# Three y writes on ScalarE's queue, one product placed behind a table, and other counts of dummy matmuls, in a three-layer token-mixing kernel

## The chip, the cores and the metric

One NeuronCore of a Trainium2 chip runs the whole program. Its engines are TensorE (PE), VectorE (DVE), ScalarE (ACT), GpSimd (POOL) and SyncE (SP, which here only issues DMAs). The metric is the device time of one execution in microseconds. A profiled execution also has a span, from its first to its last instruction.

## What is computed

Three layers follow each other, for batch 4, sequence 768, model width 384 (8 heads of 48):

```
# 1. linear attention with a decaying state, per batch and head
for t in range(S):
    y[t] = r[t] @ (state + outer(u * k[t], v[t]))
    state = w[:, None] * state + outer(k[t], v[t])
# 2. gated MLP that mixes over the sequence
h = gelu(x @ w_in);  u, v = halves of h;  v_n = layernorm(v) * g_ln
x = x + (u * (w_sg @ v_n + b_sg)) @ w_out
# 3. gated causal convolution
gate = sigmoid(sum of 5 shifted x * conv_w);  out = (gate * (x @ w_val)) @ w_out2
```

## The kernel before

The attention is done in 24 chunks of 128 tokens (6 per batch, `NCH`). Within a chunk the sum over earlier tokens is a masked score matrix; between chunks a state T is carried. Powers of the decay w stand in two tables: `tabR` weighs r and `tabK` weighs k. `tables()` builds them at the start: DVE scans powers of w and of 1/w, 64 columns long; POOL multiplies the first half of a table by its last column to get the second half (line 352 for `tabK`). From the transposed `tabK` comes `tabS`, which weighs the k that go into the state.

Of one chunk, r and k are loaded (`ld`, lines 524 to 530), v too (`lv`). POOL forms k times `tabS` (`kS`), and r times k (`dv`), then times u; DVE sums that over the head's width (`dd`), POOL multiplies v by the sum (`D`): this is the token's own term. PE transposes r and k into PSUM, DVE and ACT evacuate them (`rT`, `kT`), PE makes the scores (`S_products`, line 669) and the state's update (`KV`), and DVE masks the scores and adds to T, which ACT decays (line 720). At last PE adds three products into y (`att_Y`). For chunk 0, r times k is not in the planner's hands: `dv0` (line 587) is called in `tables()`.

y stands with channels in partitions, 112 rows with a gap. `x_rows` (line 887) brings it into the order that the MLP wants: ACT copies it from PSUM (line 900), two DMAs write its two halves to DRAM (`write`, lines 904 and 905, 48 rows of four runs of 512 bytes each), and one DMA reads it back (`read`, line 910). For batch 0 the MLP starts on each chunk when it is read back: ACT rounds it to a high part and DVE subtracts for a low part (lines 984 and 988, `X`), and the V product of that chunk can run.

The MLP's products are each three matmuls of high and low parts (`three`, lines 1091 to 1093). Its weights come as 64-bit words that ACT, DVE and POOL turn into those parts (`prepare`, lines 379 to 405, the "words" and "win" rows of the trace). `w_sg` goes through sums of squares, a scale and transposing DMAs (line 497) before the mixing product over the sequence (`mlp_SG`) can start.

The order of every engine's instructions is written out when the program is built. A planner keeps a time for each engine and for the DMA engines; each step of a chain has engines it may go to and a planned cost, and the step that can start first goes next (`next_step`), with priorities for ties. "Q" is the DMA queue: its steps all go to `nc.sync`, in the order of the planned times; for Q steps of low priority the planner keeps no more than `AHEAD` of transfer time in front. `small` is the load of `g_ln` and `b_sg` (lines 316 and 318); it may go once the r and k of chunk `AFTER_SM` are in.

Where the planner foresees that PE waits in the first 30 us, `go` puts in dummy matmuls of ones (line 222), as many as fit into the planned wait; `FILLS` can replace the count of the n-th such place. More dummies follow the first scores and the first y, and `LAST_FILL` of them follow the last product of the program. Dummies write a PSUM tile that nobody reads.

Of the kernel before, what the change touches and what calls it, by code (L numbers as in the profile page):

```python
# [24 lines left out]
Q = P // 2  # L25
# [7 lines left out]
class Kern:  # L33
# [145 lines left out]
    def go(self, streams, choose):  # L179
# [3 lines left out]
        while True:  # L183
# [9 lines left out]
            if n is None:  # L193
# [7 lines left out]
                if n:  # L201
                    self.fill(FILLS.get(self.n_fill, n))
                    self.n_fill += 1
# [116 lines left out]
    def tables(self):  # L320

        nc = self.nc
        M = Q
        self.tabR = self.const([HR, NP, P], F32, "tabR")
        self.tabK = self.const([HR, NP, P], F32, "tabK")
        self.W = self.const([HR, NP], F32, "W")
        q = self.Rst(F32)[:HR, 0:NP * (Q + 1)].rearrange("d (p n) -> d p n", p=NP)
        wq, rw = (self.const([HR, NP], F32, n) for n in ("wq", "rw"))
        t = self.Rst(F32)[:HR]
        z, y, e = (t[:, n * NP * M:(n + 1) * NP * M].rearrange("d (p n) -> d p n", n=M) for n in range(3))  # L330
        nc.gpsimd.memset(z, 0.0)
        nc.gpsimd.memset(q[:, :, 0:1], 1.0)


        nc.vector.tensor_scalar(wq, self.wP, W_LEAST, W_MOST, ALU.max, ALU.min)

        def scan(src, dst):
            for p in range(NP):
                nc.vector.tensor_tensor_scan(dst[:, p], src[:, p:p + 1].to_broadcast([HR, M]), z[:, p], 1.0, ALU.mult, ALU.add)

        scan(wq, q[:, :, 1:])
        nc.scalar.copy(self.tabR[:, :, 0:M], q[:, :, 0:M])
        nc.gpsimd.tensor_mul(self.tabR[:, :, M:], q[:, :, 0:M], q[:, :, M:].to_broadcast([HR, NP, M]))
        nc.vector.reciprocal(rw, wq)
        scan(rw, y)


        nc.vector.scalar_tensor_tensor(e, q[:, :, 1:], -1.0, y, ALU.mult, ALU.mult)
        nc.vector.scalar_tensor_tensor(self.tabK[:, :, 0:M], e, 2.0, y, ALU.add, ALU.mult)

        def second(e):
            e.tensor_mul(self.tabK[:, :, M:], self.tabK[:, :, 0:M], self.tabK[:, :, M - 1:M].to_broadcast([HR, NP, M]))
            e.tensor_mul(self.W, q[:, :, M:].rearrange("d p o -> d (p o)"), q[:, :, M:].rearrange("d p o -> d (p o)"))

        self.dv0(nc.gpsimd)
        second(nc.gpsimd)
        self.mark("tabS0", T_S)

# [313 lines left out]
    def S_products(self, i):  # L672
        nc = self.nc
        rT, kT = self.kr[i]
        pA, pB = self.ps_a(), self.ps_a()
        for p in range(NP):
            for ps, r0 in ((pA, 0), (pB, 64)):
                nc.tensor.matmul(ps[:, p * P:(p + 1) * P], kT[r0:r0 + D, p, :], rT[r0:r0 + D, p, :], start=True, stop=True)
        self.mark(("S", i))
        if not i:  # L680
            self.fill(12)
        mb = self.mask.unsqueeze(1).to_broadcast([P, NP, P])
        parts = self.scores[i] = []
        for n, ps in enumerate((pA, pB)):

            def masked(e, ps=ps):
                t = self.wp.tile([P, NP, P], F32, tag="sc", name=self.nm("sc"), bufs=2)
                e.tensor_mul(t, ps.rearrange("s (p t) -> s p t", t=P), mb)
                parts.append(t)

            self.chain(("sc", i, n), ("V", 602.0, masked, ["sc"], ["pa"]), after=[("Y", i - 1)] if i else [], prio=pr(i))
# [199 lines left out]
    def x_rows(self, i, py):  # L891

        b, c = divmod(i, NCH)
        scr = self.xd[i]
        half, q = divmod(c, 3)
        x = {}

        def evac(e):
            x["y"] = self.wp.tile([HR, NP, P], F32, tag="yT", name=self.nm("yT"), bufs=NY)
            e.copy(x["y"], py.rearrange("d (p t) -> d p t", t=P))  # L900

        def write(e):
            dst = scr.rearrange("(p j e) t -> j e p t", p=NP, j=2)
            e.dma_start(dst[0], x["y"][0:D])
            e.dma_start(dst[1], x["y"][64:HR])

        def read(e):
            if q == 0:
                self.new_xf(b, half)
            e.dma_start(self.xf[b, half][:, :, KC - 1 + q * P:KC - 1 + (q + 1) * P], scr.rearrange("(m c) t -> c m t", c=P))  # L910

        self.chain(
            ("y", b, c),
            ("A", 500.0, evac, ["yT"], ["pa"]), ("Q", (2, 600), write, [], ["yT"]), ("Q", (1, 600), read, [] if q else ["xf"]),
            after=[("y", b, c - 1)] if q else [], prio=0,
        )
        if q == 0:
            self.x_parts(b, half)
# [333 lines left out]
    def mlp_O2(self, b, half, q, dst=None):  # L1252
# [13 lines left out]
        if b == B - 1 and half:  # L1266
            if q == 2:
                pz = self.ps_m()
                for _ in range(LAST_FILL):
                    nc.tensor.matmul(pz[:, 0:P], self.onesb, self.onesb, start=True, stop=True)  # L1270
# [182 lines left out]
def pr(i):  # L1453

    return 0 if i < NCH else PR_A if i >= 2 * NCH or i < FROM_B else PR_B
# [6 lines left out]
FROM_B, PR_B = 9, 2.5  # L1462
RAW, PR_RAW = 13, 2.5
QUAD, PAST_NS = 6, 520
AFTER_SG, AFTER_SM, AFTER_CW = 6, 6, 9
WA, WM = 4, 4
NW = 3
NR, NS, NA, NX, NY, NL, NV, NPA = 12, 10, 3, 3, 2, 3, 2, 4
# [16 lines left out]
BODY = "U10 S00 U11 S01 U12 S02 U13 S03 O00 O01 O02 S10 S11 A00 A01 A02 S12 S13 P00 O10 P01 O11 P02 O12 v0 A10 u00 A11 v1 A12 v2 u01 u02 v3 u03 P10 v4 P11 P12 v5"  # L1485
END = "U10 S00 U11 S01 U12 S02 U13 S03 O00 O01 S10 S11 O02 S12 S13 A00 A01 A02 O10 O11 O12 P00 P01 A10 A11 A12 P02 P10 P11 P12"
LATER = ['a', 'a', 'a', 'a', 'a', 'a']
FILLS = {}
LAST_FILL = 5
W_LEAST, W_MOST = 0.75, 1.0  # L1490
N_OK = HR * NP

# [41 lines left out]
```

## Time and profile before

| | before |
|---|---|
| median of 3 runs | 434.7 us (433.62 to 434.74) |
| profiled execution, its time | 432.49 us |
| profiled execution, its span | 430.7 us |
| PE busy, share of the span | 411.3 us, 96% |
| DVE busy | 346.6 us, 80% |
| ACT busy | 207.1 us, 48% |
| POOL busy | 208.9 us, 49% |
| mean granted TensorE clock | 0.996 of full speed |
| packets of SP's DMA queue, share of 16 DMA engines | 46.5% |

Times of day within the span are in microseconds from its first instruction. A busy time is the union of an engine's instructions; dummies count as busy PE. Idle time before an instruction is put down to what released it last. Issuing a DMA occupies the engine whose queue issues it (SPq, ACTq), and is not counted as busy; its landing is counted from the start of the issue.

### The profile page before, as it was taken

To read this page: it belongs to the slowest core of one execution; us is meant where nothing else is said; L and a number is where in the kernel's file an instruction comes from. 1 tells how busy PE (TensorE), PEld (TensorE's weight loads), DVE (VectorE), ACT (ScalarE), POOL (GpSimd) and SP (SyncE) were. 2 spreads that over 40 slices of the span, in tenths; PEclk is the share of its full clock that TensorE was granted. 3 is DMA by queue.
4 is the path that set the end of the run, shared out by engine and by line. 5 is a ranking of instruction groups with operands and counts; after the bars stand their busy time and mean duration, and the time that the engine had idled before them with its cause. 6 is when DMAs were issued, how large, how long until landed. Compare 5 with 4: busy or idle time off the path is not lost. (4 is left out here: it accounts for less than half of the span.)

```text
span 430.7 us, 11575 instructions
## 1 busy us (share of the span) xinstructions
PE 411.3 (96%) x4616; PEld 346.9 (81%) x4616; DVE 346.6 (80%) x740; ACT 207.1 (48%) x439; POOL 208.9 (49%) x243
## 2 busy tenths in 40 slices
PE   7988998889999999999999999899999999999996
PEld 7776787857787999877887999777878989776896
DVE  6887899987899788788989799777786696649992
ACT  2546667754464486534253486532132763104152
POOL 6776976466267657673597757652110322100000
PEclk9999999989999999999999999999999999999999
DMA  6998997699646716764558541632002001000012
GB/s 164 204 237 190 256 274 188 129 198 204 171 87 133 195 47 152 175 163 107 126 124 211 148 113 37 176 84 55 20 2 91 18 2 55 2 0 2 0 38 79
DMA packets 128955, 50.15 MB, mean 116 GB/s; under 512 B 90752, under 2 KB 126720, under 8 KB 128896
## 3 DMA queue, kind: packets, MB, share of 16 engines
q1 hardware_dynamic: 128464, 48.76, 46.5%
q8 instruction: 38, 0.62, 0.6%
q10 hardware_dynamic: 432, 0.59, 0.4%
q14 instruction: 21, 0.17, 0.1%
HBM read 37.54 MB, written 9.44 MB: 109 GB/s over the span
## 5 line engine op out<-in xcount | busy, mean ns | idle before, releaser
L1091 PE MATMUL pm<-wsg,vh 128*128 128x384 f16 x192 | 63.6, 331 | 0.6 <-DVE S L1242 0.6
L1093 PE MATMUL pm<-wsg,vh 128*128 128x384 f16 x192 | 63.2, 329 | 0.0
L1092 PE MATMUL pm<-wsg,vh 128*128 128x384 f16 x192 | 63.1, 329 | 0.0
L1212 DVE SCALAR_TENSOR_TENSOR words<-xf,cw,words 128x384 f32<-128x384 f32 x72 | 44.3, 615 | 3.3 <-ACT words L1210 2.3
L1424 POOL TENSOR_TENSOR R<-S,R 128x384 fp32r<-128x384 f32 x16 | 16.0, 1008 | 56.3 <-ACT R L1450 51.2
L1424 POOL TENSOR_TENSOR ks<-kp,tabS 128x384 f32<-128x384 f32 x24 | 24.3, 1012 | 26.8 <-PE pa L783 13.4
L1091 PE MATMUL pm<-R,win 128*128 128x384 f32 x96 | 34.1, 355 | 1.0 <-ACT S L1148 1.0
L1091 PE MATMUL pm<-R,wout 128*128 128x384 f32 x96 | 33.2, 346 | 0.0
L1092 PE MATMUL pm<-R,wout 128*128 128x384 f32 x96 | 32.3, 336 | 0.1
L1093 PE MATMUL pm<-R,win 128*128 128x384 f32 x96 | 32.3, 337 | 0.0
L1092 PE MATMUL pm<-R,win 128*128 128x384 f32 x96 | 32.2, 335 | 0.0
L1093 PE MATMUL pm<-R,wout 128*128 128x384 f32 x96 | 32.2, 335 | 0.0
L1178 DVE SCALAR_TENSOR_TENSOR S<-pm,gs,b_bc 128x384 f32<-128x384 f32 x32 | 19.6, 614 | 15.2 <-PE pm L1093 13.9
L1450 ACT CAST R<-S 128x384 fp32r<-128x384 f32 x33 | 16.7, 511 | 29.3 <-DVE S L1424 14.4
L1091 PEld LDWEIGHTS <-vh 128*128 128x128 f16 x192 | 19.0, 99 | 14.5 <-issue 3.5
L1093 PE MATMUL pm<-win,R 128*128 128x512 f32 x72 | 28.7, 398 | 1.7 <-DVE R L988 1.7
L1424 POOL TENSOR_TENSOR R<-xf,R 128x384 fp32r<-128x384 f32 x12 | 12.1, 1012 | 37.0 <-ACT R L1450 21.3
L1091 PE MATMUL pm<-win,R 128*128 128x512 f32 x72 | 28.7, 398 | 0.5 <-ACT R L984 0.5
L1093 PEld LDWEIGHTS <-vh 128*128 128x128 f16 x192 | 18.9, 98 | 12.6 <-issue 0.3
L1092 PEld LDWEIGHTS <-vh 128*128 128x128 f16 x192 | 19.0, 99 | 12.0 <-issue 1.5
L1092 PE MATMUL pm<-win,R 128*128 128x512 f32 x72 | 28.4, 395 | 0.0
L1424 POOL TENSOR_TENSOR rs<-rs,exps 128x1 f32<-128x1 f32 x24 | 14.3, 597 | 29.0 <-DVE rs L1114 20.1
(196 smaller groups left out, 1226.6 us busy)
## 6 DMA issues: line engine op xcount, KB each, us to landing
rp<-in_r_dram SPq DMA_DIRECT2D x24, 192.0 KB, 3.6
kp<-in_k_dram SPq DMA_DIRECT2D x24, 192.0 KB, 4.0
v<-in_v_dram SPq DMA_DIRECT2D x24, 192.0 KB, 3.8
xd<-yT SPq DMA_DIRECT2D x48, 96.0 KB, 2.2
xf<-xd SPq DMA_DIRECT2D x24, 192.0 KB, 2.7
raw<-in_r_dram SPq DMA_DIRECT2D x43, 96.0 KB, 2.6
raw<-in_k_dram SPq DMA_DIRECT2D x43, 96.0 KB, 2.5
out_dram<-S SPq DMA_DIRECT2D x21, 192.0 KB, 1.9
```

The source lines that it names most:

```text
L1091: nc.tensor.matmul(ps, lh, rh, start=m == 0, stop=False)
L1092: nc.tensor.matmul(ps, lh, rl, start=False, stop=False)
L1093: nc.tensor.matmul(ps, ll, rh, start=False, stop=m == total - 1)
L1178: ("V", 529.0, lambda e: e.scalar_tensor_tensor(t, pg[:, :TH], self.gs[:, d:d + 1], self.b_bc[:, ts], ALU.mult, ALU.add), [], ["pm"]),
L1212: eng.scalar_tensor_tensor(t, row[:, j:j + TH], self.cw[:, e, j:j + 1], t, ALU.mult, ALU.add)
L1424: self.made.append(call(*a, **kw))
L1450: return "AV", {"A": 413.0, "V": 269.0}, lambda e: e.copy(dst, src()) if hasattr(e, "copy") else e.tensor_copy(dst, src()), [], list(give)
```

## The change

Six edits. `dv0`, POOL's r times k of chunk 0, is called between the two products of `second`, so that it stands behind the second half of `tabK` and ahead of `W`. The dummies behind the first scores go from 12 to 22. The two DMAs that write y go to ScalarE's queue (`nc.scalar`) for chunks 0, 1 and 2; in the planner the step is still a Q step with the same cost, so that its place among all instructions is found as before. `AFTER_SM` goes from 6 to 5, which lets `small` be loaded one chunk earlier. Five places of dummies in the first 11 us get other counts. The dummies behind the last product go from 5 to 16.

```diff
         def second(e):
             e.tensor_mul(self.tabK[:, :, M:], self.tabK[:, :, 0:M], self.tabK[:, :, M - 1:M].to_broadcast([HR, NP, M]))
+            self.dv0(e)
             e.tensor_mul(self.W, q[:, :, M:].rearrange("d p o -> d (p o)"), q[:, :, M:].rearrange("d p o -> d (p o)"))
 
-        self.dv0(nc.gpsimd)
         second(nc.gpsimd)
...
         if not i:
-            self.fill(12)
+            self.fill(22)
...
-            ("A", 500.0, evac, ["yT"], ["pa"]), ("Q", (2, 600), write, [], ["yT"]), ("Q", (1, 600), read, [] if q else ["xf"]),
+            ("A", 500.0, evac, ["yT"], ["pa"]), (("Q", (2, 600), lambda e: write(self.nc.scalar), [], ["yT"]) if i < Y_ACT else ("Q", (2, 600), write, [], ["yT"])), ("Q", (1, 600), read, [] if q else ["xf"]),
...
-AFTER_SG, AFTER_SM, AFTER_CW = 6, 6, 9
+AFTER_SG, AFTER_SM, AFTER_CW = 6, 5, 9
...
-FILLS = {}
-LAST_FILL = 5
+FILLS = {7:8,8:2,9:3,10:1,13:3}
+LAST_FILL = 16
+Y_ACT = 3
```

## Rows read from the trace of the kernel before

**Rows 1.** Stretches of the span: busy time and count of each engine, clock, DMA share

```profile
14.00:28.40 14.40, 12.55 (x181) 10.52 (x178) 11.44 (x22) 7.34 (x19) 11.66 (x13) 1.00 0.89 194
28.40:60.00 31.60, 29.11 (x333) 24.54 (x333) 26.41 (x60) 20.84 (x50) 23.07 (x28) 1.00 0.92 250
60.00:90.00 30.00, 24.64 (x349) 21.03 (x348) 28.09 (x73) 21.94 (x56) 17.30 (x22) 0.99 0.76 163
90.00:426.60 336.60, 333.60 (x3606) 280.49 (x3606) 271.12 (x560) 152.23 (x308) 147.92 (x157) 1.00 0.38 94
```

**Rows 2.** The tables at the start: DVE's scans by form, instructions in order of time

```profile
L339 DVE TENSOR_TENSOR_SCAN Rst<-wq,Rst 112x64 f32<-112x64 f32 x4 | 0.8, 274 | 0.3 <-POOL Rst L332 0.3
...
5.96 1.05 DVE L339 TENSOR_TENSOR_SCAN Rst<-rw,Rst 112x64 f32<-112x64 f32 x1
...
5.86 1.01 POOL L589 TENSOR_TENSOR dv<-rp,kp 128x384 f32<-128x384 f32 x1
...
8.19 0.61 POOL L352 TENSOR_TENSOR tabK<-tabK 112x256 f32<-112x256 f32 x1 [1.33 <-DVE tabK L349]
```

**Rows 3.** What the first chunks wait for, in order of time (start, duration)

```profile
10.45 0.51 ACT L379 ACTIVATE words<-Rst 128x384 f32<-128x384 f32 x1 [0.47 <-DMA Rst<-in_moe_w_in_dram]
...
11.00 0.57 DVE L1424 TENSOR_SCALAR words<-words 128x384 int32<-128x384 int32 x1 [0.29 <-ACT words L379]
...
11.85 0.84 PE L222 MATMUL warm<-onesb 128*128 128x128 bf16 x12
...
12.69 0.56 PE L705 MATMUL pa<-v,ks 128*48 128x48 f32 x16
...
15.83 1.03 POOL L1424 TENSOR_TENSOR dv<-rp,kp 128x384 f32<-128x384 f32 x1 [1.14 <-DMA kp<-in_k_dram]
```

**Rows 4.** SP's issues in order of time; then line 905's issue times (min/median/max, ns)

```profile
16.18 1.56 SPq L530 DMA_DIRECT2D kp<-in_k_dram  x1
...
19.42 1.89 SPq L904 DMA_DIRECT2D xd<-yT  x1
...
28.40 1.87 SPq L904 DMA_DIRECT2D xd<-yT  x1
...
37.39 3.05 SPq L316 DMA_DIRECT2D g<-in_moe_g_ln_dram  x1
...
L905 SPq DMA_DIRECT2D xd<-yT x6: 436/540/783, 21.4 to 64.1; - x6
```

**Rows 5.** The last DMA issue on ScalarE's queue

```profile
427.16 0.34 ACTq L1271 DMA_DIRECT2D out_dram<-S  x1
```

**Rows 6.** ACT and DVE around the first y write

```profile
16.68 0.50 ACT L405 CAST win<-S 128x384 fp32r<-128x384 f32 x1
...
19.06 0.35 DVE L714 TENSOR_TENSOR T<-pa,T 48x192 f32<-48x192 f32 x1 [0.25 <-PE pa L705]
```

**Rows 7.** ACT, DVE and PE around the second y write, in order of time

```profile
28.87 0.39 ACT L720 ACTIVATE T<-T,W 112x112 f32<-112x112 f32 x1 [0.49 <-DVE T L714]
...
30.90 0.51 ACT L379 ACTIVATE words<-Rst 128x384 f32<-128x384 f32 x1
...
31.51 0.55 DVE L1424 TENSOR_SCALAR words<-words 128x384 int32<-128x384 int32 x1
...
34.86 0.56 PE L705 MATMUL pa<-v,ks 128*48 128x48 f32 x16 [0.66 <-DMA v<-in_v_dram]
...
35.54 0.35 DVE L714 TENSOR_TENSOR T<-pa,T 48x192 f32<-48x192 f32 x1 [0.50 <-PE pa L705]
```

**Rows 8.** Chunk 7: landing of r and k issued at 36.3 and 36.8; k's first later use

```profile
DMA to landing us min/median/max: 5.0/5.2/5.3
...
46.60 1.01 POOL L1424 TENSOR_TENSOR ks<-kp,tabS 128x384 f32<-128x384 f32 x1
```

**Rows 9.** PE and its clock just before and after 89 us; columns as in Rows 1

```profile
86.00:89.00 3.00, 0.91 (x40) 0.81 (x33) 2.61 (x8) 1.36 (x5) 2.02 (x3) 1.00 0.97 77
89.00:93.00 4.00, 4.00 (x18) 1.97 (x17) 3.69 (x6) 4.00 (x9) 2.51 (x3) 0.57 1.18 236
```

## The prediction

> **What bounds the kernel now.** The busy shares of the page say "PE", but they average over stages, so the first view to read is the table of stretches [rows 1]. From 90.0 to 426.6 us PE is busy for 333.6 of 336.6 us: whatever the change does there, only 3 us of idle PE could be won, and no edit but the last one lies in that stretch. So the end is the moment at which PE enters that stretch, plus a constant. Before it, three stretches show different limits. From 60 to 90 DVE works 28.1 of 30 us. From 28.4 to 60 DVE works 26.4 and PE 29.1 of 31.6 us, with the DMA engines 92% busy. From 14 to 28.4 POOL works 11.7, DVE 11.4 and PE 12.6 of 14.4 us (part of PE's are dummies), with the DMA engines 89% busy. No engine is alone in front before 90: the order on four engines, each in a written order, sets the pace. An edit counts only if it moves DVE, since DVE's work up to 90 us is the same before and after and DVE is the fullest from 60 on.
>
> The second view was the instructions in order of time with their idle time, for 5 to 36 us; the third SP's issues; the fourth the clock by stretch. I take the parts in that order.
>
> **r times k behind the table.** POOL's product ran from 5.86 to 6.87, and one of DVE's scans of the 1/w powers took 1.05 us in just that time, where four scans of the same size took 0.27 us each [rows 2]. With the product gone from there the scan should take 0.27: 1.05 - 0.27 = 0.78 us off DVE's way to `tabK`, so the second half of `tabK` starts at 7.4 instead of 8.19, and the first scores about 0.8 us sooner. The product then runs at about 8.0 to 9.0 on POOL, followed by W (0.2 us), ahead of POOL's next step, which started at 9.35: nothing is late. But the gain goes no further: DVE's next step, at 11.00, waits for ACT's first "words", and that waited at 10.45 for the landing of the first w_in, a DMA which nothing here moves [rows 3]. DVE's queue behind it (sums, mask of the scores) starts from there, and a second gate stands at 15.83, where POOL waited 1.14 us for chunk 1's k [rows 3]. Worth 0; if the w_in landing were no gate, at most 0.78 us.
>
> **Dummies.** The 29 dummies that ended at 7.31 become 14, and those between the transposes and the scores 14 -> 9 (the planned waits at those places give 18, 5, 5, 2 and 7, replaced by 8, 2, 3, 1 and 3). They are what has to be taken away for the scores to start sooner; by themselves they delayed nothing. The 22 behind the scores cost 0.84/12 = 0.07 us each, 1.54 us [rows 3]. If the scores end at 11.1 instead of 11.9, the dummies end at 12.7, where the first state product started (12.69): cost 0. If the scores are not earlier they end at 13.4, 0.7 us too late, which the 1.14 us of POOL's wait covers. LAST_FILL: 11 more dummies add at most 0.8 us to PE after its last product, beside the last copy and the last write, which was issued at 427.16 and ends the span at 430.7 [rows 5]: cost 0.
>
> **`small` one chunk earlier.** By the planner's rule this load goes ahead of chunk 7's r and k instead of behind them. It holds SP for 3.05 us and about 0.5 more [rows 4]; chunk 7's loads are next in the queue, then `w_out`, v of chunk 5 and y of chunk 3, which stood behind `small` before as well. Chunk 7's k was issued at 36.8 and landed 5.3 us later, at 42.1; 3.6 us more is 45.7, still ahead of its use at 46.60 [rows 8]. Cost 0, with 0.9 us to spare; without SP's relief below the spare is all there is.
>
> **y of chunk 0 on ACT's queue.** SP loses 1.89 + 0.44 = 2.3 us of issue time at 19.42 [rows 4]. The loads behind it (chunks 4 and 5, the read of y, w_in) move up, but no engine waits for one of them before 28.4. On ACT the two issues stand behind the "words" step and ahead of the rounding at 16.68. What an issue costs on ACT is the unknown of this change: the only ones in the trace took 0.34 us, at the end with idle DMA engines [rows 5]; the same two on SP took 2.33. I take 2 x 0.34 = 0.7 us: SP's long issues come where its own queue has loads in front, and ACT's queue is empty. Then ACT's rounding ends at 17.9 rather than 17.2, DVE's step behind it comes some 0.2 us late, and the 0.25 us that DVE waited at 19.06 [rows 6] take that in. Cost 0; at 2.33 us it is about 1.5 us of DVE (ACT free at 19.1, the step at 17.8 starts at 19.5, and DVE has 0.25 idle behind it).
>
> **y of chunk 1.** SP loses 1.87 us and about half a microsecond [rows 4]. This is the part with something on the path. PE waited 0.66 us at 34.86 for v of chunk 3, and through PE, DVE waited 0.50 at 35.54 [rows 7]. That v may not be issued before the first y of chunk 1 is finished, so it is not issued sooner; it lands sooner because the three w_in loads in front of it go out about 2 us sooner. At best DVE's 0.50 us are gone: -0.50. Against that, ACT issues two DMAs behind its decay at 28.87 (0.39 us long, under which the first issue can hide): 0.68 - 0.39 = 0.29 us later for the "words" at 30.90, which ended 0.1 us ahead of DVE's use at 31.51 [rows 7]. DVE is full from there to 35.54. So -0.50 + 0.29 = **-0.2 us**. Ends: -0.66 (PE's whole wait, ACT's issues hidden) and +1.9 (2.33 us on ACT, v not sooner).
>
> A rule of the Trainium skill speaks against the gain. The DMA engines are 89 and 92% busy in these stretches [rows 1]. The Trainium skill's page "DMA: Bandwidth & Descriptors", section "Issuing engines are not separate DMA queues", says that DMAs of several engines run on the same 16 DMA engines and that a second issuer saves only the issue time. By it v would land no sooner, and this part would be +0.3 rather than -0.2; no row here shows a write from ACT beside SP's loads.
>
> **y of chunk 2.** On SP it was issued late in a quiet moment; on ACT some 0.7 us among steps that have over 1 us of idle time between them. 0.
>
> **Sum.** 0 + 0 + 0 + 0 - 0.2 + 0 = -0.2 us on a span of 430.7. The profiled execution took 432.49, 1.8 above its span; the median of the runs, 434.7, is 2.2 above that. Same offsets: 434.5 us.
>
> **Rivals.** *A: ACT is held by the issues (slower).* SP was issuing k of chunk 3 from 16.18 to 17.74 [rows 4], the moment at which ACT would issue. If the two cannot issue at once, or ACT's issue slows with the load as SP's did, each of the first two pairs holds ACT about 2.3 us. Price: 1.5 us at the first, 1.4 at the second (2.33 - 0.39 - 0.50 of DVE idle): +2.9, 437.6 us; half of that, 436.1, if one pair is held. It decides from about 1 us of ACT per pair on. For it: the DMA load. Against: the queue of its own. The Trainium skill's page "Perfetto Trace Analysis", section "DMA Instruction — HWDGE (DVE, Sync)", has the descriptor generator locked for exclusive use, which is this rival; no trace here shows it.
>
> *B: the stall before 89 us changes (faster).* PE is busy only 0.91 of the 3 us up to 89, and then the granted clock is 0.57 of full on average from 89 to 93, with a part at 1.2 GHz, where PE is full: 4 x 0.43 = 1.7 us lost [rows 9]. An order that reaches 89 us otherwise, DVE having won the 0.5 to 0.7 us above and SP's reads and loads being 2 to 4 us earlier, can close enough of that idle time to keep the clock: -1.7 - 0.7 = -2.4, 432.3 us. Against: the idle time there follows DVE's and ACT's own order, not a load.
>
> *C: the first table counts after all.* If the w_in landing moves or is not the gate, -0.8: 433.9 us, within what I call the same.
>
> *D: the change does not do what it says:* if the scan does not shorten, the 22 dummies are late by 0.7 us; covered, 434.5 us.
>
> **How the numbers follow.** Forecast with D 0.37, C 0.08, A 0.23, B 0.32. A measurement of this kernel can tell about 0.3%, 1.3 us, from no change. So faster 0.32 (B), same 0.45, slower 0.23 (A). The range reaches B on one side and most of A on the other, where only both pairs held at full price lie outside: 432.0 to 437.0.
>
> **What would show it.** In the new profile: the slow scan at 0.27 us and the second half of `tabK` at about 7.4; DVE's "words" still at 11.0 and POOL's product of chunk 1 still at 15.8; ACT's issues in rows of their own (0.3 us each: the forecast; 1 us and more: A); PE's wait for v at 34.9 gone; `small` ahead of chunk 7's loads; the clock after 89 us (at full: B). Wrong if PE reaches the first mixing product by more than 1 us sooner or later than at 89.6 without a change of the clock there: then a load or an issue that I call covered was on the path.

## The result and the profile after

The changed kernel takes 436.42 us (median of 15 runs, 434.94 to 437.99), the kernel before 434.17 us on the same chip (432.32 to 437.09). The ratio is 1.0055, with a 95% interval of 1.0037 to 1.0074: 2.4 us slower, where 434.5 us and no difference that can be measured had been forecast. The time lies inside the range (432.0 to 437.0), but that is luck: the range was drawn for two rivals of which neither is what made the kernel slower. Two executions of the kernel with 16 dummies alone, and one of the kernel before beside the last run below, fell into a slower state of the chip; medians count them, ratios leave them out.

The profiled execution took 436.52 us, with a span of 434.7 (before: 432.49 and 430.7) and a mean clock of 0.990 (0.996).

**The start.** Instructions in order of time (start, duration, in brackets the idle time ahead and what ended it):

```profile
5.18 1.21 DVE L339 TENSOR_TENSOR_SCAN Rst<-rw,Rst 112x64 f32<-112x64 f32 x4
...
7.39 0.61 POOL L352 TENSOR_TENSOR tabK<-tabK 112x256 f32<-112x256 f32 x1 [1.51 <-DVE tabK L349]
7.96 1.02 POOL L589 TENSOR_TENSOR dv<-rp,kp 128x384 f32<-128x384 f32 x1
...
10.81 0.52 ACT L379 ACTIVATE words<-Rst 128x384 f32<-128x384 f32 x1 [1.64 <-DMA Rst<-in_moe_w_in_dram]
...
11.37 0.57 DVE L1424 TENSOR_SCALAR words<-words 128x384 int32<-128x384 int32 x1 [1.47 <-ACT words L379]
```

The slow scan is gone (four now take 1.21 us together, where one alone took 1.05 [rows 2]), and the second half of `tabK` starts 0.80 us sooner. Then ACT waits 1.64 us for the first w_in, where it waited 0.47 [rows 3]: all of it is given back at that gate. That step of ACT started 0.36 us later in this execution; its start varies from 10.43 to 11.35 us over the traces of this study.

**y on ScalarE's queue, and `small`.** Same columns:

```profile
16.72 0.43 ACTq L904 DMA_DIRECT2D xd<-yT  x1
17.19 0.73 ACTq L905 DMA_DIRECT2D xd<-yT  x1
...
17.97 0.51 ACT L405 CAST win<-S 128x384 fp32r<-128x384 f32 x1 [0.85 <-ACT words L379]
...
18.51 0.56 DVE L1424 TENSOR_TENSOR win<-S,win 128x384 fp32r<-128x384 f32 x1 [0.27 <-ACT win L405]
...
29.31 0.31 ACTq L904 DMA_DIRECT2D xd<-yT  x1
29.66 0.46 ACTq L905 DMA_DIRECT2D xd<-yT  x1
...
34.75 0.56 PE L705 MATMUL pa<-v,ks 128*48 128x48 f32 x16 [0.16 <-DVE sc L688]
...
35.44 0.48 SPq L316 DMA_DIRECT2D g<-in_moe_g_ln_dram  x1
...
36.99 1.07 SPq L530 DMA_DIRECT2D kp<-in_k_dram  x1
38.10 3.04 SPq L391 DMA_DIRECT2D Rst<-in_moe_w_out_dram  x1
```

An issue costs ACT 0.31 to 0.73 us, a pair 0.8 to 1.2, where SP spent 1.87 and 1.89 on the first of a pair [rows 4]. PE's wait of 0.66 us for v [rows 7] is gone; the 0.16 left are for DVE. But that wait belongs to one execution: the seven other traces of this study in which SP writes y do not have it either. The same place with 16 closing dummies as the only edit:

```profile
34.77 0.56 PE L705 MATMUL pa<-v,ks 128*48 128x48 f32 x16
```

`small` stands ahead of chunk 7's r and k, and its first load holds SP for 0.48 us instead of 3.05. The hold did not go away, it moved: the load of `w_out` behind took 3.04 us to issue, where before it took 0.43:

```profile
41.04 0.43 SPq L391 DMA_DIRECT2D Rst<-in_moe_w_out_dram  x1
```

So it is in all traces: with `small` at its old place it takes 1.6 to 3.05 us and `w_out` 0.43 or 0.44 (eight traces), with `small` earlier it takes 0.48 and `w_out` 1.5 to 3.0 (six). How long an issue took on SP tells here where SP was held, and not what that DMA costs.

**Around 89 us.** Stretches of the span (length, busy time and count of PE, PEld, DVE, ACT, POOL, clock, DMA share, GB/s):

```profile
86.00:89.00 3.00, 0.91 (x53) 0.82 (x46) 2.40 (x8) 1.51 (x4) 2.03 (x3) 0.83 0.73 140
89.00:93.00 4.00, 4.00 (x16) 2.66 (x16) 3.68 (x7) 3.80 (x8) 2.74 (x3) 0.50 1.02 215
93.00:97.00 4.00, 4.00 (x101) 2.51 (x103) 2.57 (x4) 0.71 (x3) 1.53 (x2) 0.78 1.02 222
```

PE's idle time of some 2 us before 89 is as it was; behind it the lower clock (1.2 GHz) holds longer than in [rows 9]: 6.8 us, from 87.96 to 94.79, against 3.4, from 89.36 to 92.78. The 3.4 us more at half the clock, with PE full for most of them, are worth up to 1.7 us, and PE ended its last product 1.73 us later than before, at 428.35 instead of 426.62. That is of this execution: with the same five edits and 5 closing dummies the lower clock held for 3.4 us. The span ended 4.0 us later, so 2.3 us more came after PE's last product.

**The end.** First the instructions in order of time:

```profile
428.01 0.34 PE L1093 MATMUL pm<-w_out,R 128*128 128x384 f32 x1
...
428.19 1.07 PE L1270 MATMUL pm<-onesb 128*128 128x128 bf16 x16
428.39 0.48 ACT L1271 COPY S<-pm 128x384 f32<-128x384 f32 x1 [1.08 <-PE pm L1093]
428.90 0.34 ACTq L1271 DMA_DIRECT2D out_dram<-S  x1
```

The closing lines of the program by engine (line, engine, operation: duration in ns, when):

```profile
L1503 PEldq TENSOR_LOAD <-n_ok x1: 781/781/781, 427.9 to 427.9; - x1
...
L1504 ACTq COMPARE_BRANCH  x1: 54/54/54, 430.1 to 430.1; - x1
...
L1504 PEldq COMPARE_BRANCH  x1: 4362/4362/4362, 428.7 to 428.7; - x1
```

The issue of the last write (KB, us to landing), and the DMA queues from 430.43 to 432.60 (packets, MB, share of 16 engines):

```profile
out_dram<-S ACTq DMA_DIRECT2D x1, 192.0 KB, 4.2
...
q8 instruction: 1, 0.02, 2.8%
q10 hardware_dynamic: 9, 0.01, 2.5%
```

PE's closing lines in the kernel before:

```profile
L1502 PEldq TENSOR_LOAD <-n_ok x1: 492/492/492, 424.2 to 424.2; - x1
...
L1503 PEldq COMPARE_BRANCH  x1: 3638/3638/3638, 424.8 to 424.8; - x1
```

The program ends with a test that the front part leaves out: each engine loads `n_ok`, a count of decays that the fast path can handle, and branches past a general path that is run only where the count is short. On ACT the branch takes 0.05 us. On PE it takes 3.6 us before and 4.4 after, and a packet of an instruction queue (q8, 16 KB) moves in that time. In all 13 traces that have the test PE's branch ends 1.3 to 1.4 us after that packet. PE's sequencer comes to the load while PE still has queued matmuls: before, 2.4 us ahead of the end of the last product (424.2 against 426.62), so that the branch lay beside real work. With 16 dummies the load stands at 427.9, 0.5 us ahead of 428.35, and the branch runs until 433.1. In that time falls the last write, and it lands 4.2 us after its issue. SP waits for that landing (until 433.07, 4.7 us after the last product; before until 429.04, 2.4 us after it) and in both kernels needs 1.7 us more to close the program.

### The profile page after: what moved, and what is told of

Its sections match the earlier page's. It is cut to its first block, busy times and chain, and to the rows that moved or that the text cites. A ratio compares the mean times of both kernels' runs of the same rounds, so it can differ in the third digit from the quotient of the medians.

```text
span 434.7 us, 11573 instructions
## 1 busy us (share of the span) xinstructions
PE 413.6 (95%) x4617; PEld 348.9 (80%) x4617; DVE 346.7 (80%) x740; ACT 206.5 (47%) x439; POOL 208.5 (48%) x243
## 5 line engine op out<-in xcount | busy, mean ns | idle before, releaser
L1092 PE MATMUL pm<-win,R 128*128 128x512 f32 x72 | 28.4, 395 | 0.0
```

The costliest lines, as they stand in the source:

```text
L1092: nc.tensor.matmul(ps, lh, rl, start=False, stop=False)
```

## The experiments

All are timed against the kernel before, beside it on one chip. Its medians were 436.16 us for the first four runs below, 434.35 for those with 32 dummies and with single edits, 434.65 for ten dummies, no test and the first of the two on the clock, and 435.47 for the last. "Tail" is the time from the end of the last product to the end of the span of the profiled execution: in the kernel before 430.71 - 426.62 = 4.09 us, in the changed one 434.74 - 428.35 = 6.39.

**All but the last edit.**

```diff
-LAST_FILL = 16
+LAST_FILL = 5
```

> The changed kernel with 5 closing dummies, as before the change; its other five edits stay. Theory 1 (the closing dummies hold PE's last branch: the branch began at 424.8, before PE's last product, in the old trace and at 428.75, behind it, in the new one): the tail from the end of the last product to the end of the span goes back from 6.4 to about 4.1 us, and the time is within 1 us of the kernel before (ratio 0.998 to 1.002). Theory 2 (the y writes and the start cost the time): the tail is short again but the ratio stays near 1.005, with PE's first mixing product about 1 us later than in the kernel before. Theory 3 (the stall before 89 us keeps the clock low for longer in the new order): ratio 1.002 to 1.005, with two stretches of low clock where the kernel before has one.

434.4 us, ratio 0.9964 (0.9931 to 0.9997), tail 4.09. Without that one number the loss is gone. The ratio is below what theory 1 expected, and the lowest of all versions that compute everything, but its interval ends just under 1 and overlaps those of most other runs.

**The last edit alone**, in the kernel before:

```diff
-LAST_FILL = 5
+LAST_FILL = 16
```

> The kernel before with 16 closing dummies and no other edit. Theory 1: the whole loss, ratio 1.004 to 1.007, a tail of about 6.4 us, and PE's closing branch beginning near the end of the last product. Theories 2 and 3: no difference to the kernel before, beyond 0.8 us that the dummies take on PE if something waits for them.

438.63 us, ratio 1.0052 (1.0016 to 1.0089), tail 6.31. The whole change lost as much (ratio 1.0055, tail 6.39): the loss is in this edit.

**Fewer but longer dummies**, in the kernel before: 4 of 512 columns instead of 5 of 128. They keep PE busy for 1.04 us, the 16 short ones for 1.07.

```diff
-                for _ in range(LAST_FILL):
-                    nc.tensor.matmul(pz[:, 0:P], self.onesb, self.onesb, start=True, stop=True)
+                for _ in range(4):
+                    nc.tensor.matmul(pz, self.wsg[0][:, 0, 0:P], self.wsg[0][:, 0, 0:FF], start=True, stop=True)
```

> The kernel before with 4 closing dummies of 512 columns in place of 5 of 128: about 0.9 us of PE time, as much as 16 narrow ones, but one instruction fewer than before. If the count of instructions behind the last product is what delays the branch (theory 1): tail about 4.1 us, ratio 1.000 within 0.002. If PE's time behind the last product counts: a tail of 4.6 to 6.4 us, ratio 1.001 to 1.006.

436.45 us, ratio 0.9996 (0.9961 to 1.0032), tail 4.14. PE worked for as long as on the 16 short dummies and nothing was lost: what counts is the number of its instructions.

**No closing dummies**, in the kernel before (`LAST_FILL = 0`).

> The kernel before without closing dummies. Theory 1: PE's branch begins some 0.9 us earlier still than in the kernel before; there the last write's landing ended the span, so nothing is won: ratio 1.000 within 0.002, tail 4.1 us. If the tail went on getting shorter with fewer dummies, the branch would have been the end before as well: ratio 0.997.

435.42 us, ratio 0.9979 (0.9941 to 1.0017), tail 4.19. Below five there is nothing more to win: the last copy, its write and the closing steps set the end.

**More of it**, in the kernel before (`LAST_FILL = 32`).

> The kernel before with 32 closing dummies instead of 5, nothing else changed. Theory 1 (PE's sequencer runs a nearly fixed number of queued matmuls, 18 to 19, ahead of PE, so each further short dummy puts its load of the counter and its closing branch later against the last product, and beyond some ten of them the branch ends the span): with 32 the load starts 13 to 14 dummies of 0.067 us behind the last product, +0.9 us, where it was -0.45 us with 16 and -2.4 us with 5; the stretch from the end of the last product to the end of the span grows from 4.1 (5 dummies) and 6.35 (16) to about 7.7 us, and the time is 3.6 us over the kernel before. Rival (the closing branch costs its 4.3 us once and for all as soon as PE's queue is no longer empty when the last copy is done, whatever the count): the stretch stays at 6.4 us, +2.3. Rival (PE's own end decides, its dummies lasting 2.1 us): the span ends 2.1 - 1.07 = 1.1 us later than with 16, 7.4; the place of the load against the last product tells it from theory 1.

435.53 us, ratio 1.0026 (1.0002 to 1.005), tail 6.09. The load of the counter stood 0.7 us behind the last product (expected +0.9), but the tail did not rise to 7.7 nor the time by 3.6 us: my theory lacked something. The rows show what. With 32, the branch comes later still (430.5 to 434.3), its instruction packet starts only when the last write is over, and that write lands after 1.9 us (PE's branch, the last write, SP's waits with their sum, count and longest):

```profile
L1503 PEldq COMPARE_BRANCH  x1: 3758/3758/3758, 430.5 to 430.5; - x1
```

```profile
out_dram<-S ACTq DMA_DIRECT2D x1, 192.0 KB, 1.9
```

```profile
SPq L1530 <- PEq L1503: 2.0, 1, 2.0
```

Here SP has finished its wait for the write and waits 2.0 us for PE's branch. With 16 the branch and the write collide, and both are late. (With none, the packet lies beside the two writes before the last, and the branch takes 4.26 us too.) In the three traces with these long branches the packet starts 1.5 to 2.0 us after the branch, in the ten others 1.0 to 1.3.

**Ten**, in the kernel before (`LAST_FILL = 10`).

> The kernel before with 10 closing dummies instead of 5. With 0, 4, 5 and 16 the load of the counter stood at -3.2, -2.5, -2.4 and -0.45 us from the end of the last product. Theory 1 (18 to 19 queued matmuls ahead of PE's end): about -1.4 us with 10; the branch follows 0.55 us later and takes 3.5 to 4.4 us, and the closing steps 1.6 us more, so that the stretch behind the last product is 4.3 to 5.1 us, between the 4.1 of 5 dummies and the 6.35 of 16; time +0.2 to +1.0 us. Rival (an on-off effect between a queue that is empty and one that is not at the last copy): 4.1 or 6.4, nothing between.

435.62 us, ratio 1.0011 (0.9984 to 1.0038), tail 4.88: in the interval expected, not on or off. The load stood 1.5 us ahead of the end of the last product. Here too the write was held, by less: it landed after 2.6 us.

**No closing test**: the changed kernel with its 16 dummies, and these lines left out, so that no engine loads the counter or branches (it leaves out the general path):

```diff
-        n_ok = tc.nc.values_load(kern.n_ok, min_val=0, max_val=N_OK, skip_runtime_bounds_check_because="a count of so many comparisons")
-        with tc.If(n_ok < N_OK):
-            kern.general(x_scr)
```

> The changed kernel with its 16 closing dummies, without the load of the counter and the closing test; it leaves out the general path that the test guards, so that no engine loads or branches at the end. Theory 1, sharpened (PE's branch to the end of the program, in which each trace shows a 16 KB instruction fetch, is what ends the span; the dummies matter only because they put it later): the stretch from the end of the last product to the end of the span falls from 6.4 to about 4.1 us, where the last write's landing ends it, with the 16 dummies still there; the time is 2.3 us under the changed kernel's, at or below the kernel before, ratio 0.994 to 1.000. Rival (the 16 dummies themselves hold the end, by PE's own work or by what they do to the last copy): the stretch stays near 6.4 us, ratio 1.003 to 1.008.

432.84 us, ratio 0.9954 (0.9934 to 0.9975), tail 3.50. The 16 dummies are still there and harmless: the last write lands after 1.9 us, and SP waits for landings of writes and for nothing of PE's but 0.6 us at the very end. The tail is shorter than the 4.1 us expected because SP's closing steps behind the landing took 1.1 us here instead of 1.7 (PE in order of time, then SP's waits):

```profile
428.16 1.07 PE L1270 MATMUL pm<-onesb 128*128 128x128 bf16 x16
```

```profile
SPq L1528 <- DMA out_dram<-S: 6.2, 2, 4.7
```

The runs together (load: start of PE's load of the counter against the end of the last product; write: issue to landing):

| closing dummies | load, us | PE's branch, us | last write, us | tail, us | ratio |
|---|---|---|---|---|---|
| 0 | -3.3 | 4.26 | 2.0 | 4.19 | 0.998 |
| 4 long | -2.5 | 3.82 | 1.9 | 4.14 | 1.000 |
| 5 (all but last) | -2.4 | 3.62 | 1.9 | 4.09 | 0.996 |
| 10 | -1.5 | 3.72 | 2.6 | 4.88 | 1.001 |
| 16 (last edit alone) | -0.5 | 4.26 | 4.1 | 6.31 | 1.005 |
| 16 (changed kernel) | -0.5 | 4.36 | 4.2 | 6.39 | 1.006 |
| 16, no test | none | none | 1.9 | 3.50 | 0.995 |
| 32 | +0.7 | 3.76 | 1.9 | 6.09 | 1.003 |

How far the sequencer runs ahead can be counted: in each of the 13 traces with the test, 17 matmuls start after PE's load of the counter has started. With no closing dummies these are 17 products; with 5, 12 products and the dummies; with 16, the last product (428.01 above) and the dummies; with 32, the last 17 dummies. (The expectations reckon the lead from times, as 18 to 19.) A product starts every 0.173 us and a short dummy every 0.056, so the same 17 instructions are long in time where they are products and short where they are dummies.

Why does the write wait? In the changed kernel its last nine packets moved after 430.43 (q10 in the fence on the end), in the run with 16 alone also nine, after 431.92. Nine is a sixteenth of the write's 144, the share of one DMA engine of sixteen, and by the packets' own times the first of the nine starts when the instruction packet ends, at 431.77. In the run with five, that packet was over (427.80 to 428.98) before the write was issued at 429.09. The trace has sixteen landing signals for each of these writes: in the changed kernel fifteen of the last write's came by 430.75 and one at 433.06. So the reading is that the fetch of 16 KB holds one DMA engine, and the nine packets that are queued there hold the end. The trace does not name the engine of a packet, and no run moved the fetch alone to another one. Two things are open: why the write's share waits from the start, when the fetch of about 1 us sets in only 1.9 us after the issue, and why PE's branch alone has such a packet. The Trainium skill's page "Runtime: NRT & Kernel Launch", section "Instruction fetch mechanics", says that a taken branch to code that has not been prefetched forces a DMA fetch of the target page before execution goes on. The 16 KB packet within PE's branch in each of the traces with the test agrees with it.

**The other edits one by one**, in the kernel before. First the start: `dv0` between the products, 22 dummies behind the scores, the five other counts.

> The kernel before with only the first r times k behind the table and the dummies ahead of the first scores changed (8, 2, 3, 1 and 3 dummies, 22 behind the scores; 5 at the end as before). Theory 1: the scan takes 0.3 us, the second half of the table starts at about 7.4 us, and the first step that waits for the first w_in's landing (ACT's words) still starts at 10.4 to 10.8, so nothing is won: 0, ratio 0.997 to 1.003; the stretch behind the last product stays at 4.1 us. Rival (the first table counts): -0.8 us, with the words at 9.7. Rival (fewer dummies let the clock fall in the first 12 us): a granted clock under 1.00 there, and slower by 0.3 us or more.

432.99 us, ratio 0.9984 (0.9963 to 1.0004). Nothing that can be told from no change; the words started at 11.03, later than before and than expected.

The y writes:

```diff
-... ("Q", (2, 600), write, [], ["yT"]), ...
+... (("Q", (2, 600), lambda e: write(self.nc.scalar), [], ["yT"]) if i < 3 else ("Q", (2, 600), write, [], ["yT"])), ...
```

> The kernel before with only the first three chunks' y written by ScalarE's queue. Theory 1: this edit moves the time by nothing that can be measured, -0.2 us as forecast (436.2 becomes about 436.0, ratio 0.997 to 1.002): PE's wait of 0.66 us for v of chunk 3 at 34.9 goes, ACT holds 0.8 to 1.2 us for each pair of issues beside its own work, and the stretch behind the last product stays at 4.1 us. Rival (ACT's issues are what made the changed kernel slower): +1 us or more, to be seen as DVE's waits on ACT at 18 and 31 us.

434.75 us, ratio 1.0015 (0.9992 to 1.0038). In the trace the step that the y writes were to move came sooner: PE's product that waits for DVE's low part of x stood at 42.91, before at 43.03, although this execution's words had started 0.34 us later. That is -0.46 us up to there against this one trace of before, but it does not hold over all of them. From the start of ACT's words to that product the eight traces with y on SP's queue took 31.6 to 32.6 us (before is the longest), the six with y on ACT's 32.1 to 33.1: no gain, rather half a microsecond lost. The time shows no gain either. Single executions are also too coarse for an effect of this size: this one had a second stretch at the lower clock that the trace of before has not. 275 to 285 us, first before, then this run:

```profile
275.00:285.00 10.00, 10.00 (x113) 8.28 (x117) 7.67 (x18) 3.67 (x7) 7.17 (x8) 1.00 0.40 121
```

```profile
275.00:285.00 10.00, 9.48 (x43) 8.39 (x44) 6.22 (x16) 3.68 (x7) 5.55 (x7) 0.83 0.44 131
```

0.17 of 10 us are 1.7 us of PE's work, more than all that these edits are worth, and it comes in some executions and not in others.

The load of `small`, `AFTER_SM = 5`:

> The kernel before with only the load of the small vectors one chunk earlier. Theory 1: it changes places with chunk 7's r and k in SP's queue and nothing waits for it: 0, ratio 0.996 to 1.004, the stretch behind the last product 4.1 us. Rival (in the kernel before, where SP still issues y, its 3 us of issue make chunk 7's k late for its use at 46.6): POOL waits for k there, +0.5 to +2 us.

434.78 us, ratio 1.0008 (0.9976 to 1.0041), tail 4.10. No engine waits for chunk 7's k; the load of `w_out` behind took 2.80 us to issue.

**The clock behind the wait before 89 us.** Two kernels put 30 dummies there, in the changed kernel with 5 closing ones.

```diff
             for p in range(NP):
                 nc.tensor.transpose(...)
...
+            if i == 9 and not n:
+                self.fill(30)
```

> The changed kernel with 5 closing dummies and 30 more dummies ahead of the transposes that stand at 88.8 us, where PE waited 2.09 us in each trace so far. If the clock's fall behind that wait costs what the low stretches say (3.4 to 6.8 us at half, during which PE is full: 1.7 to 3.4 us), the granted clock stays at 1.00 from 86 to 97, and the time is 1.7 us or more under the kernel before, ratio 0.988 to 0.996, also under the 0.9964 of the same kernel without these dummies. Rival (the fall comes from something else, the end of a heavy stretch or the start of the next): the clock falls as before, and the dummies cost 0 to +0.3 us.

439.22 us, ratio 1.0095 (1.0064 to 1.0127). This was my mistake: the dummies' tile is one of the products' PSUM buffers, and a late use keeps it from them; PE waited 2.58 us at 60.7 and 1.77 us at 83.7 for buffers. The second kernel takes a buffer on the spot:

> The changed kernel with 5 closing dummies and 30 dummies ahead of the transposes at 88.8 us, now in a buffer taken there and given back at once (in the run before, the dummies' old buffer was held from 30 us on, and PE waited 2.58 us at 60.7 and 1.77 us at 83.7 for buffers of its products). If the clock's fall behind the 2.09 us wait is what costs 1.7 to 3.4 us there: PE works through 86.3 to 88.4 us on dummies, the clock stays at 1.00 from 86 to 97, no new waits before 86, and the time is 1.7 us or more under the kernel before, ratio 0.988 to 0.996. Rival (the fall does not come from the wait, or the clock falls elsewhere for it): ratio 0.996 to 1.000, like the same kernel without these dummies.

436.55 us, ratio 1.0022 (0.9991 to 1.0054), above both intervals expected. The clock held, and PE later waited for DVE; stretches first, then PE's wait:

```profile
86.00:89.00 3.00, 2.93 (x94) 2.70 (x94) 2.40 (x7) 1.51 (x4) 1.94 (x2) 1.00 0.72 140
89.00:93.00 4.00, 3.56 (x24) 2.38 (x25) 3.69 (x8) 3.34 (x7) 3.19 (x4) 1.00 1.25 197
93.00:97.00 4.00, 4.00 (x141) 3.00 (x140) 4.00 (x9) 1.40 (x4) 1.92 (x3) 1.00 1.09 212
```

```profile
113.73 0.32 PE L1095 MATMUL pm<-wsg,vh 128*128 128x384 f16 x1 [1.74 <-DVE xf L1202]
```

It is tempting to read that wait as the price of the kept clock, but it is not shown: four traces in which the clock fell at 89 (0, 4 long, 10 and 16 dummies in the kernel before) have a wait of 1.5 to 2.8 us at the same place. With the four long ones:

```profile
113.51 0.32 PE L1091 MATMUL pm<-wsg,vh 128*128 128x384 f16 x1 [2.03 <-DVE xf L1198]
```

In this execution the lower clock came at 279 to 283 us instead. One more trace kept the full clock here, that of the run without the test (there it had been low at 74 to 78):

```profile
89.00:93.00 4.00, 4.00 (x30) 2.63 (x34) 3.69 (x8) 3.63 (x8) 2.90 (x3) 1.00 0.80 162
```

From its first mixing product (89.88) to the end of its last product PE took 338.4 us there, before (from 89.61) 337.0. So neither trace turned the kept clock into time won; where it went is open.

## Why the prediction was wrong

**The step that failed** is the one on `LAST_FILL`: "11 more dummies add at most 0.8 us to PE after its last product, beside the last copy and the last write [...]: cost 0". The 0.8 us and the cover were right for PE as an engine (1.07 us for 16 instead of 0.45 for 5, over at 429.3, and the copy beside it). What I left out is that PE also has a sequencer with work of its own at the end, the load and the branch, that this work had been covered by queued matmuls, and that eleven more of them, short ones, use up that cover. For the 22 early dummies the prediction also says what they cost if they come late (0.7 us) and what covers that; for these it looked at PE's matmuls alone. The two rows of the kernel before that stand above had to be read: a branch of 3.6 us on PE that ended only 0.6 us before SP's last wait did. The term measured +2.3 us in the tail, where 0 stood in the sum. The prediction's sign of being wrong did not catch it, since it looked only at the way into the long stretch: PE's first mixing product started at 90.55 instead of 89.61, within the 1 us allowed.

**Tables and early dummies**: scan, second half of the table and the gate at the first w_in came as forecast, worth 0 (ratio 0.9984, interval across 1).

**y of chunk 0**: ACT's two issues took 1.20 us rather than 0.68. ACT's rounding started at 17.97 and ended at 18.48 (forecast end 17.9; 0.36 us are the late start of the words), and DVE waited 0.27 us for it. At 34.75 nothing is left of that against the trace of before.

**y of chunk 1**: 0.81 us on ACT rather than 0.68; ACT's words at 31.80 (before 30.90, of which 0.36 are the late start). PE's wait for v and DVE's 0.50 us behind it are gone, but not through this edit: v landed 6.9 us after its issue in the one trace that was read, 4.9 to 5.8 us in the seven others with y on SP's queue, which have no wait for it, and 4.5 to 6.2 us with y on ACT's. So the -0.2 us rested on a wait of one execution, and on issue times that move to another load when a load is taken away (k at 29.95 now took 2.68 us to issue, before 1.52 at 31.46). The run with this edit alone measured +0.15% (-0.08 to +0.38%). The rule of the Trainium skill that was weighed there (page "DMA: Bandwidth & Descriptors", section "Issuing engines are not separate DMA queues") says that a second issuer saves only issue time. No run here speaks against it.

**`small`, y of chunk 2**: 0, as forecast.

**Rival A** (ACT held 2.3 us a pair) is false at its price: no pair took more than 1.20 us, though the first is just over the 1 us from which the prediction let it count. ACT's issues at 16.72 and 17.19 fell into one of SP's:

```profile
16.77 2.41 SPq L530 DMA_DIRECT2D v<-in_v_dram  x1
```

The locked descriptor generator of the Trainium skill's page "Perfetto Trace Analysis" (section "DMA Instruction — HWDGE (DVE, Sync)") does not show here as a hold of ACT.

**Rival B** did not come about: PE's idle time ahead of 89 stayed at 2.09 us, and the clock fell as before, and for longer. Its price is not borne out either: in the two traces that kept the clock up there, PE came to the end of its last product no sooner.

**The sum**: five edits forecast at -0.2 us measured -0.36% (-0.69 to -0.03%), about -1.6 us, for which the three single runs (-0.16, +0.15 and +0.08%) give no owner; the sixth forecast at 0 measured +0.52% (0.16 to 0.89%), +2.3 us. The direction of the whole was set by the term at 0 without a range of its own; the one term that was not 0, y of chunk 1, showed no gain in its own run.

## What to carry to other kernels

An instruction put behind the last useful one is not free because its engine is done: look at what that engine's sequencer still has to do (loads of registers, branches, closing semaphores) and at how much queued work lies over it. Count instructions there, not time: four long dummies cost nothing where sixteen short ones of the same length cost 2.3 us. A cost set at 0 because it is covered needs the end of the cover beside it, from a row. And a gain forecast from a wait needs that wait in more than one execution.

## What the runs showed of the hardware

When PE's load of the counter started, 17 matmuls were still to start, in each of 13 traces with 0 to 32 closing dummies. The branch behind it took PE 3.5 to 4.4 us, with a 16 KB instruction packet in it, and the other engines 0.05 to 0.07 us. One such packet at the moment of a 192 KB write raised the write's landing from 1.9 to 4.2 us, with one of sixteen landing signals late. A DMA issue of y on ACT's queue took 0.31 to 0.73 us with the DMA engines some 95% busy (0.96 of 14 to 28.4 us, 0.95 of 28.4 to 60). An issue on SP's took up to 3.05 us, and when that DMA was moved, the hold fell on another one's issue. Single executions of the same instructions differ by stretches of 3.4 us at the lower clock, worth up to 1.7 us each: in 11 of 14 traces at the end of PE's wait of 2.1 us before 89 or soon behind it (in the changed kernel's for 6.8 us), in five behind one of 1.7 us at 273 to 278.
